# Softmax exponentials on ScalarE without a bias operand, and the matching constant on VectorE

## The chip, the cores and the metric

The kernel runs on one core of one Trainium2 chip. The metric is the device time of one execution in microseconds. The five engines of the core go by the names of the profile: PE (TensorE, matrix products), ACT (ScalarE, activations), DVE (VectorE), POOL (GpSimd) and SP (SyncE, which here only issues transfers). Each engine runs its own queue in order and waits on semaphores for the others. Matrix products are written to PSUM; everything else on the core lives in SBUF.

## The reference

The result is a gated mix of two branches over the same input x (2048 rows, 512 columns, bf16):

```python
x = A_x
g = sigmoid((x * gate_w).sum(-1, keepdims=True))
a = attention(x, A_wqkv, A_wo)
b = state_space(x, B_A_re, ..., B_Dskip)
return g * a + (1 - g) * b

# attention: H = 32 heads of Dh = 16
q, k, v = (x @ wqkv) split into heads
scores = einsum("bhqd,bhkd->bhqk", q, k) * Dh ** -0.5
p = softmax(scores)
o = einsum("bhqk,bhkd->bhqd", p, v);  a = o @ wo

# state_space: per channel d a kernel of 2048 taps, summed over N = 128 complex modes,
K[d, l] = Re(sum_n C[d, n] * exp(dt[d] * A[d, n] * l) * dt[d] * B[d, n])
# convolved causally with the channel of x, plus x * Dskip
```

The scores of 32 heads, 2048 queries and 2048 keys are 134 million exponentials. The change concerns these alone.

## The kernel before, in words

**The attention.** The work is cut into 32 blocks: four chunks of 512 queries, times four sets of eight heads, times the even or the odd heads of a set. In a block four heads are worked on together, and the 2048 keys are taken in 16 tiles of 128. One head, one key tile and 512 queries make a *slot*: 128 x 512 scores, one PSUM bank. There are 2048 slots.

Slots are taken in groups. `qk` (L691) multiplies keys and queries of up to three slots into one of two PSUM tiles of three banks, SC0 and SC1, by turns. `ex` (L704) lets ACT turn two or three of these banks into exponentials in SBUF (ET), as one instruction of 128 x 1024 or 128 x 1536. A group in which ACT takes two banks has a third slot whose exponential DVE computes: `exp_in` (L715) reads the bank, and `exp_out` (L722) ends the work in SBUF (ED). 60 of the 2048 slots go this way. `pv` (L740) multiplies the exponentials of four slots, from ET or from ED, with the values, and adds them up in the PSUM tile OA over the 16 key tiles of a block. The values carry a column of ones, so the same product gives the sum of the exponentials; at a block's end DVE transposes OA and divides by that sum (`norm_a`, `norm_b`, `norm_c`). A factor common to all exponentials of a row thus drops out, but ACT's and DVE's exponentials must have the same factor.

**DVE's exponential.** It writes x / ln 2 as a number whose bits are, read as a float, roughly 2 to that power (L718, into eL as an integer). The mantissa of eL, made into a number m from 1 to 2 (L728), goes into a cubic that corrects the straight line between powers of two (L731, L733, L735). The cubic is worked out with its leading factor POLY[0] divided away, so DVE's result was too large by -1 / (8 * POLY[0]) = ESC = 1.174. ACT's exponential was given the same factor by a bias of ln ESC, which DVE writes once into the tile lnc (L636) and ACT reads as one value for each partition.

**The state space branch and the rest.** The parameters, tables of powers, a chunked scan over 32 chunks of 64 rows and products with it, the gate and the output projection run on DVE, PE and SP between the groups of the attention. Their small products share one PSUM tile, MB, which DVE empties.

**What sets the order.** A planner in the program (`Sched`) writes out the order of each queue before launch. It walks through the groups, charges ACT 0.063 + 0.4267 n us for a group of n slots (L709), and fills the time of PE, DVE, SP and POOL until then with other work by priority. When PE would have too little work, it adds products of zeros (OA<-wm, L1426) up to a budget per group. Buffers get their SBUF addresses at the end, by their size and time of life (`place`, L486). At run time every queue keeps this order.

So a group goes round as follows: PE's `qk` waits until ACT has read the tile of the group before last; ACT's `ex` waits for `qk`; meanwhile PE does `pv` of earlier groups and the other branch's products.

Of the kernel before, what the change touches and what calls it, by code (L numbers as in the profile page):

```python
# [6 lines left out]
FP32 = mybir.dt.float32  # L7
BF16 = mybir.dt.bfloat16
INT32 = mybir.dt.int32
AF = mybir.ActivationFunctionType  # L10
# [6 lines left out]
DH = 16  # L17
# [11 lines left out]
CYCLE, LOWS = 30, 24  # L29
EDGE = 384  # L30
POLY = (-0.10644581, 0.70747665, -1.37730927, 1.77561576)
ESC = -1 / (8 * POLY[0])
EW = 2
VW = 152

# [27 lines left out]
class Prog:  # L63
# [104 lines left out]
    def op(self, eng, fn, R=(), W=(), c=.1, lat=.05, a=0):  # L168
        if self.cap is not None:
            self.cap.append((self.op, (eng, fn, R, W), dict(c=c, lat=lat, a=a)))  # L170
            return
        self.act += a
        self.log.append((self.op, self.q, (eng, fn, R, W)))
        deps = self._deps(eng, R, W)
        i = self.cnt[eng]
        at = self.tm[eng]
        for s, k in deps.items():
            at = max(at, self.fin[(s, k)] + (0 if s == eng else .08))
        self.tm[eng] = at + c
        self.fin[(eng, i)] = at + c + lat  # L180
        self.cnt[eng] += 1
        self._record(eng, fn, deps, eng, i, R, W)
        return at + c + lat
# [197 lines left out]
def declare(nc, es):  # L381
    B = {}

    def sb(name, free, dt=BF16):
        B[name] = Buf(name, "sb", free, dt)


    sb("KT", 4 * S)
    for k in range(16):
        sb(f"Q{k}", 512)  # L390
        sb(f"OnT{k}", 512)
    sb("Qm", 2 * 512)
    sb("VE", 64 * VW)
    sb("ET", NS * 512)
    sb("OT", 512, FP32)
    sb("ON", 512)
    sb("Rz", 2 * 16, FP32)
    sb("Wo", 4 * D)
    sb("xT", 4 * S)
    for n in ("Wk", "Wq", "Wv"):  # L400
        sb(n, 4 * D)
    sb("msk", 2, FP32)
    sb("sgn", 2, FP32)
    sb("hm", 2, FP32)
    sb("piota", 4, FP32)
    sb("hpi", 1, FP32)
    sb("lnc", 1, FP32)
    for k in range(EW):
        sb(f"eL{k}", 512, FP32)
    sb("em", 512, FP32)  # L410
    sb("eu", 512, FP32)
    sb("ED", 4 * 512)

    sb("gwT", 4)
    sb("wm", D)
    sb("x0n", 4 * D)
    sb("idf", P, FP32)
    sb("idb", P)
    sb("gp", NCH, FP32)
    sb("ge", NCH, FP32)  # L420
    sb("g", NCH, FP32)
    sb("g1", NCH, FP32)
    sb("Dpb", 16)
    sb("Dp", 16, FP32)
    sb("Yl", 16 * D)
    sb("fo", 4 * D)
    sb("fp", 4 * D, FP32)

    for n in ("AreT", "AimT", "BreT", "BimT", "CreT", "CimT", "ldt", "dt"):
        sb(n, D)  # L430
    for n in ("an", "bn", "ba", "ea", "e2", "sb_", "cb", "u1", "u2", "u3", "u4", "zr", "zi"):
        sb(n, D, FP32)
    sb("wrb", D)
    sb("nwi", D)
    sb("VV", 2 * D, FP32)
    sb("VL", 2 * D, FP32)
    for n in ("L1", "L2", "L4", "L8", "L16", "L32", "L48"):
        sb(n, 2 * D, FP32)
    sb("MU", 3 * D, FP32)
    sb("pt1", 2 * D, FP32)  # L440
    sb("pt2", 2 * D, FP32)
    for n in ("D16", "D32", "D48"):
        sb(n, 2 * 2 * D)

    sb("FP", 2 * 128 * 8, FP32)
    sb("ft1", 2 * 64 * 8, FP32)
    sb("ft2", 2 * 64 * 8, FP32)
    for k in range(4):
        sb(f"B16{k}", 2 * 128 * 16)

    sb("PT", 2 * 2 * CB * T)
    sb("tt1", 2 * CB * 16)
    sb("tt2", 2 * CB * 16)
    sb("Qt", 2 * 32 * 128)
    sb("Kst", 2 * 8 * P)

    for k in range(NSG):
        sb(f"SG{k}", NCH * 2 * SGH)
    sb("G", 2 * 128, FP32)
    for n in ("s2", "s3"):  # L460
        sb(n, 2 * 128, FP32)

    for k in range(4):
        sb(f"X2{k}", 32 * 64)
        sb(f"XZ{k}", 2 * 32 * 64)
        sb(f"XS{k}", 32 * 64)
        sb(f"XP{k}", 32 * 64)
        sb(f"XR{k}", 32 * 64)

    sb("Py", 3 * 2 * 16 * T)  # L470
    sb("Tt", 3 * 8 * 128)
    for i in range(2):
        B[f"SC{i}"] = Buf(f"SC{i}", "ps", 1536, FP32)
    B["OA"] = Buf("OA", "ps", 512, FP32)
    B["MB"] = Buf("MB", "ps", 512, FP32)
    for n, free in (("ptd", NBLK * P * 2 * CB * T), ("kpd", NBLK * P * 8 * P), ("xrd", S * D)):
        B[n] = Buf(n, "dr", free, BF16)
        B[n].t = nc.dram_tensor("gm_" + n, [free // P, P], BF16)
    for n in ("SC0", "SC1", "OA", "MB"):
        B[n].t = es.enter_context(nc.psum_tensor(n, [P, B[n].free], FP32))  # L480
    for n in ("x", "w", "wo", "are", "aim", "bre", "bim", "cre", "cim", "ldt_d", "dsk_d", "gw_d", "out"):
        B["d_" + n] = Buf("d_" + n, "dr", 1, BF16)
    return B
# [52 lines left out]
def build(nc, A_x, A_wqkv, A_wo, B_A_re, B_A_im, B_B_re, B_B_im, B_C_re, B_C_im, B_log_dt, B_Dskip, gate_w, out):  # L536
    ins = dict(x=A_x.flatten_outer_dims().tensor, w=A_wqkv.tensor, wo=A_wo.tensor, are=B_A_re, aim=B_A_im, bre=B_B_re,
               bim=B_B_im, cre=B_C_re, cim=B_C_im, ldt=B_log_dt.tensor, dsk=B_Dskip.tensor, gw=gate_w.tensor,
               out=out.flatten_outer_dims().tensor)
    with ExitStack() as es:  # L540
        bufs = declare(nc, es)
        prog = Prog(bufs)
        for b in bufs.values():
            b.over, b.order = (), 0
        record(nc, prog, bufs, ins)
        place(nc, bufs)
        log = prog.log
        prog = Prog(bufs)
        for f, q, a in log:
            prog.q = q  # L550
            (prog.op if f.__name__ == "op" else prog.dma)(*a)
        prog.emit(nc, es)
# [10 lines left out]
def record(nc, p, B, ins):  # L563
    KT, Qm, VE, ET, OT, ON, Rz = (B[n] for n in ("KT", "Qm", "VE", "ET", "OT", "ON", "Rz"))
# [4 lines left out]
    op, dma = p.op, p.dma  # L569
    NQ = 512  # L570
    NSL = 4 * NQ
    OFF, GRP, RING, OWN = [], [], {}, {}
# [60 lines left out]
    for k in range(9):  # L633
        mm(lambda: OA(0, [[1, 512]]), lambda: wm(0, [[1, 128]]), lambda: wm(0, [[1, 512]]), [(wm, 0)], [(OA, 0, "warm")])
    op("DVE", lambda v: v.memset(hpi(0, [[1, 1]]), HALF_PI), [], [(hpi, 0)])
    op("DVE", lambda v: v.memset(B["lnc"](0, [[1, 1]]), math.log(ESC)), [], [(B["lnc"], 0)])  # L636
    op("DVE", lambda v: v.memset(pio(1, [[1, 1]]), 0.0), [], [(pio, 1)])
    for k in range(1, 8):
        op("DVE", lambda v, k=k: v.scalar_tensor_tensor(
# [64 lines left out]
    def ex(g):  # L704
        at, d = GRP[g]
        sc, e, n = SC[g % 2], RING[at[0]], len(at)
        op("ACT", lambda a: a.activation(ET(512 * e, [[1, 512 * n]]), sc(0, [[1, 512 * n]]), AF.Exp, scale=DH ** -0.5,  # L707
                                         bias=B["lnc"](0, [[1, 1]])),
           [(sc, i, g) for i in range(n)] + [(B["lnc"], 0)], [(ET, RING[s], s) for s in at], c=.063 + .4267 * n, lat=.1)  # L709

    em, eu, ED = (B[n] for n in ("em", "eu", "ED"))
    r2, r1, r0 = (POLY[i] / POLY[0] for i in (1, 2, 3))
    one = [[1, 512]]

    def exp_in(k, g, d):  # L715
        eL, sc, i = B[f"eL{k % EW}"], SC[g % 2], len(GRP[g][0])
        yield ("DVE", .68, -2)
        op("DVE", lambda v: v.tensor_scalar(eL.int(0, one), sc(512 * i, one), DH ** -0.5 / math.log(2) * 2 ** 23, 124.0 * 2 ** 23 - 2.0 ** 31,  # L718
                                            ALU.mult, ALU.add), [(sc, i, g)], [(eL, 0, d)], c=.68)
        sch.mark(f"ei{k}")  # L720

# [49 lines left out]
    def key(*ns):  # L771
        return [(B[n], 0) for n in ns]
# [588 lines left out]
    for q4 in range(4):  # L1361
        sc = SC[1] if q4 < 3 else MB
# [8 lines left out]
        else:  # L1371
# [6 lines left out]
                                     bias=hpi(0, [[1, 1]])), key("ba") + [(hpi, 0)], key("cb"), c=.6)  # L1378
# [79 lines left out]
    def compose():  # L1458
# [31 lines left out]
        if d is not None:  # L1490
            sch.add(exp_in(nd, g, d), 1)
            sch.add(exp_out(nd, d), 1)
            nd += 1
# [5 lines left out]
    g = 0  # L1499
    while True:  # L1500
        p.q = g
        for s in GRP[g][0]:
            if RING[s] in OWN:
                sch.force(f"pv{OWN[RING[s]] // 4}")
            OWN[RING[s]] = s
        ex(g)
        sch.mark(f"g{g}")
        sch.mark(f"blk{at_slot(GRP[g][0][0])[2]}")
        more = compose()
        if more:  # L1510
            need(g + 1)
            qk(g + 1)
        t = p.tm["ACT"]
        sch.fill(t, .5, zeros, want, quiet())
        lack[0] = max(min(lack[0] + budget() - p.act, 384), 0)
        p.act = lack[1] = 0
        if not more:
            break
        g += 1
# [53 lines left out]
```

## Time and profile before

| what | value |
|---|---|
| median of 3 runs | 991.09 us (981.5 to 995.3) |
| the profiled execution, its own time | 984.66 us |
| its span, first to last instruction | 982.9 us |
| mean granted PE clock | 0.959 |
| busy: ACT | 960.6 us (98%) |
| busy: DVE | 811.3 us (83%) |
| busy: PE | 791.3 us (81%) |
| ACT's exponentials (L707) | 683 instructions, 953.4 us |
| of these 128 x 1536 / 128 x 1024 | 622 / 61 |
| DVE's first pass (L718) | 60 instructions, 41.2 us |

The span lies 1.8 us under the time of its execution. Busy time is the union of an engine's instructions; on ACT and PE neighbouring instructions overlap in the record, so a mean duration is longer than the time from one to the next. A group is named by its source line, engine and operation, then the tiles written <- read, shapes and types, and the count; behind the bar stand busy time, mean duration in ns, and the idle time of the engine just before, with what ended it. All matrix products are issued by one helper line, L578.

### The profile page before, as it was taken

To read this page: it belongs to the slowest core of one execution; us is meant where nothing else is said; L and a number is where in the kernel's file an instruction comes from. 1 tells how busy PE (TensorE), PEld (TensorE's weight loads), DVE (VectorE), ACT (ScalarE), POOL (GpSimd) and SP (SyncE) were. 2 spreads that over 40 slices of the span, in tenths; PEclk is the share of its full clock that TensorE was granted. 3 is DMA by queue.
4 is the path that set the end of the run, shared out by engine and by line. 5 is a ranking of instruction groups with operands and counts; after the bars stand their busy time and mean duration, and the time that the engine had idled before them with its cause. 6 is when DMAs were issued, how large, how long until landed. Compare 5 with 4: busy or idle time off the path is not lost.

```text
span 982.9 us, 17954 instructions
## 1 busy us (share of the span) xinstructions
PE 791.3 (81%) x7409; PEld 269.6 (27%) x7521; DVE 811.3 (83%) x1654; ACT 960.6 (98%) x693; POOL 14.6 (1%) x16
## 2 busy tenths in 40 slices
PE   7888887878777787777888888887788888888884
PEld 3233232212222222212232222323223233333321
DVE  5799989997667888898988788888888987778885
ACT  6999999999999999999999999999999999999995
POOL 4000000000000000010000000000000000000000
PEclk7999999988999989989999779999999999999998
DMA  8300000016767556471242266335312232201100
GB/s 187 87 1 1 1 1 1 1 22 166 178 162 171 151 144 99 133 210 21 55 103 54 58 94 98 83 74 105 58 28 61 79 98 56 55 7 28 33 1 22
DMA packets 171473, 73.40 MB, mean 75 GB/s; under 512 B 150272, under 2 KB 159104, under 8 KB 169344
## 3 DMA queue, kind: packets, MB, share of 16 engines
q1 hardware_dynamic: 169088, 71.07, 31.0%
q10 hardware_dynamic: 2304, 1.18, 0.6%
q8 instruction: 59, 0.97, 0.4%
q14 instruction: 22, 0.18, 0.1%
HBM read 30.02 MB, written 25.17 MB: 56 GB/s over the span
## 4 chain that ended last, share of the span: by engine, by line
ACT 93%; PE 4%; DMA 1%; DVE 1%; issue 0%; ACTq 0%; DVEq 0%
ACT ET L707 93%; PE OA L578 2%; PE SC L578 2%; DMA Wq<-in_A_wqkv_dram 1%; PE MB L578 0%; DVE fo L1253 0%; ACTq L582 0%; DVE OT L752 0%; DVE OnT L762 0%; DVE KT L668 0%; ACT e L826 0%; ACT ea L824 0%; DVE ON L757 0%; DVE Rz L756 0%; ACT ge L1230 0%
## 5 line engine op out<-in xcount | busy, mean ns | idle before, releaser
L707 ACT ACTIVATE ET<-SC,lnc 128x1536 bf16<-128x1536 f32 (+1 forms) x683 | 953.4, 1832 | 6.1 <-PE SC L578 5.6
L578 PE MATMUL SC<-Qm,KT 32*128 32x512 bf16 x2048 | 276.4, 398 | 158.7 <-ACT ET L707 146.0
L578 PE MATMUL OA<-wm 128*128 128x512 bf16 (+9 forms) x684 | 223.3, 374 | 15.4 <-issue 12.8
L578 PE MATMUL OA<-ET,VE 128*32 128x512 bf16 x1988 | 203.9, 402 | 1.8 <-DVE OT L752 1.0
L578 PEld LDWEIGHTS SC<-Qm,KT 32*128 32x128 bf16 x2048 | 66.8, 91 | 382.5 <-ACT ET L707 366.4
L578 PEld LDWEIGHTS OA<-ET,VE 128*32 128x32 bf16 x1988 | 51.0, 94 | 125.0 <-issue 118.3
L578 PEld LDWEIGHTS OA<-wm 128*128 128x128 bf16 x785 | 55.7, 98 | 86.9 <-issue 73.3
L718 DVE TENSOR_SCALAR eL<-SC 128x512 int32<-128x512 f32 x60 | 41.2, 688 | 38.3 <-PE SC L578 38.0
L766 DVE TENSOR_TENSOR tt<-B,D 128x1024 bf16<-128x1024 bf16 x96 | 62.4, 684 | 0.5
L1054 DVE TENSOR_TENSOR SG<-MB,sgn 128x496 bf16<-128x496 f32 x64 | 43.0, 671 | 19.2 <-PE MB L578 18.7
L1087 DVE TENSOR_TENSOR G<-s,s 128x256 f32<-128x256 f32 x120 | 50.7, 423 | 3.3
L578 PE MATMUL MB<-SG,Py 128*64 128x32 bf16 x1024 | 50.9, 230 | 0.0
L1083 DVE TENSOR_TENSOR s<-s,SG 128x256 f32<-128x256 f32 x120 | 50.3, 419 | 0.0
L1077 DVE TENSOR_TENSOR s<-G,MU 128x256 f32<-128x256 f32 x120 | 50.2, 418 | 0.0
L1080 DVE TENSOR_TENSOR s<-G,MU 128x256 f32<-128x256 f32 x120 | 50.2, 418 | 0.0
L735 DVE SCALAR_TENSOR_TENSOR ED<-eu,eL 128x512 bf16<-128x512 f32 x60 | 41.4, 689 | 1.3
L733 DVE SCALAR_TENSOR_TENSOR eu<-eu,em 128x512 f32<-128x512 f32 x60 | 41.3, 688 | 1.4
L752 DVE STREAM_TRANSPOSE OT<-OA 128x512 f32<-128x512 f32 x32 | 22.9, 717 | 23.5 <-PE OA L578 23.0
L731 DVE SCALAR_TENSOR_TENSOR eu<-em 128x512 f32<-128x512 f32 x60 | 41.1, 686 | 0.9
L578 PEld LDWEIGHTS MB<-SG,Py 128*64 128x64 bf16 x1024 | 30.7, 117 | 28.6 <-issue 28.5
L1090 DVE CAST SG<-G 128x256 bf16<-128x256 f32 x120 | 35.4, 295 | 3.2
L766 DVE TENSOR_TENSOR ft<-FP,L 128x1024 f32<-128x1024 f32 (+1 forms) x32 | 34.2, 1086 | 0.4
(137 smaller groups left out, 566.1 us busy)
## 6 DMA issues: line engine op xcount, KB each, us to landing
gm_ptd<-PT SPq DMA_DIRECT2D x16, 1024.0 KB, 5.9
Py<-gm_ptd SPq DMA_DIRECT2D x32, 512.0 KB, 4.1
gm_kpd<-Kst SPq DMA_DIRECT2D x16, 256.0 KB, 3.8
Tt<-gm_kpd SPq DMA_DIRECT2D x128, 32.0 KB, 3.4
gm_xrd<-in_A_x_dram SPq DMA_DIRECT2D x1, 2048.0 KB, 12.1
XS<-gm_xrd SPq DMA_DIRECT2D x8, 256.0 KB, 4.3
XR<-gm_xrd SPq DMA_DIRECT2D x8, 256.0 KB, 4.4
out_dram<-fo SPq DMA_DIRECT2D x28, 64.0 KB, 2.1
```

The lines of the kernel that those rows point to most:

```text
L578: op("PE", lambda t: t.matmul(out(), lhsT(), rhs(), start=start, stop=stop, skip_group_check=True, **kw), R, W, c=c, lat=.15, a=a)
L707: op("ACT", lambda a: a.activation(ET(512 * e, [[1, 512 * n]]), sc(0, [[1, 512 * n]]), AF.Exp, scale=DH ** -0.5, bias=B["lnc"](0, [[1, 1]] ...
L718: op("DVE", lambda v: v.tensor_scalar(eL.int(0, one), sc(512 * i, one), DH ** -0.5 / math.log(2) * 2 ** 23, 124.0 * 2 ** 23 - 2.0 ** 31, A ...
L731: op("DVE", lambda v: v.scalar_tensor_tensor(eu(0, one), em(0, one), r2, em(0, one), ALU.add, ALU.mult), key("em"), key("eu"), c=.69)
L733: op("DVE", lambda v: v.scalar_tensor_tensor(eu(0, one), eu(0, one), r1, em(0, one), ALU.add, ALU.mult), key("em", "eu"), key("eu"), c=.69)
L735: op("DVE", lambda v: v.scalar_tensor_tensor(ED(512 * (d % 4), one), eu(0, one), r0, eL(0, one), ALU.add, ALU.mult), key("eu") + [(eL, 0, ...
L766: op(eng, lambda v: v.tensor_tensor(o(), a(), b_(), f), R, W, c=c)
L1054: op("DVE", lambda v, bank=bank: v.tensor_tensor(sg(2 * SGH + CB * bl + 8 * bank, [[2 * SGH, 31], [SGH, 2], [1, 8]]), MB(0, [[1, 31], [256 ...
L1077: op(e, lambda v: v.tensor_tensor(s2(0, [[128, 2], [1, 128]]), G(0, [[128, 2], [1, 128]]), MU(d0, [[0, 2], [1, 128]]), ALU.mult), key("G", ...
L1080: op(e, lambda v: v.tensor_tensor(s3(0, [[128, 2], [1, 128]]), G(128, [[-128, 2], [1, 128]]), MU(D + d0, [[D, 2], [1, 128]]), ALU.mult), k ...
L1083: op(e, lambda v, so=so: v.tensor_tensor(s2(0, [[128, 2], [1, 128]]), s2(0, [[128, 2], [1, 128]]), sg(so, [[SGH, 2], [1, 128]]), ALU.add), ...
L1087: op(e, lambda v: v.tensor_tensor(G(0, [[1, 256]]), s2(0, [[1, 256]]), s3(0, [[1, 256]]), ALU.add), [(s2, 0), (s3, 0)], [(G, 0)], c=.38)
```

## The change: the factor moves from ACT to DVE

ACT's exponential loses its bias: it computes exp(s x) and no longer exp(s x + ln ESC). The tile lnc and the instruction that fills it go. DVE's first pass adds a constant to the exponent; this constant now holds log2(-8 * POLY[0]) besides 124, so DVE's result is smaller by the factor 1.174 and again agrees with ACT's. The number of instructions on ACT and in DVE's exponential, their shapes and the planner's charges are as before.

```diff
-ESC = -1 / (8 * POLY[0])
+EXP0 = (124 + math.log2(-8 * POLY[0])) * 2 ** 23 - 2.0 ** 31
...
-    sb("lnc", 1, FP32)
...
-    op("DVE", lambda v: v.memset(B["lnc"](0, [[1, 1]]), math.log(ESC)), [], [(B["lnc"], 0)])
...
     def ex(g):
         at, d = GRP[g]
         sc, e, n = SC[g % 2], RING[at[0]], len(at)
-        op("ACT", lambda a: a.activation(ET(512 * e, [[1, 512 * n]]), sc(0, [[1, 512 * n]]), AF.Exp, scale=DH ** -0.5,
-                                         bias=B["lnc"](0, [[1, 1]])),
-           [(sc, i, g) for i in range(n)] + [(B["lnc"], 0)], [(ET, RING[s], s) for s in at], c=.063 + .4267 * n, lat=.1)
+        op("ACT", lambda a: a.activation(ET(512 * e, [[1, 512 * n]]), sc(0, [[1, 512 * n]]), AF.Exp, scale=DH ** -0.5),
+           [(sc, i, g) for i in range(n)], [(ET, RING[s], s) for s in at], c=.063 + .4267 * n, lat=.1)
...
     def exp_in(k, g, d):
-        op("DVE", lambda v: v.tensor_scalar(eL.int(0, one), sc(512 * i, one), DH ** -0.5 / math.log(2) * 2 ** 23, 124.0 * 2 ** 23 - 2.0 ** 31,
+        op("DVE", lambda v: v.tensor_scalar(eL.int(0, one), sc(512 * i, one), DH ** -0.5 / math.log(2) * 2 ** 23, EXP0,
                                             ALU.mult, ALU.add), [(sc, i, g)], [(eL, 0, d)], c=.68)
```

## The prediction

> **What bounds the kernel now.** I read the page first: the busy time of the engines, the chain that ended last by engine, and the costliest group.
>
> ```profile
> span 982.9 us, 17954 instructions
> ...
> PE 791.3 (81%) x7409; PEld 269.6 (27%) x7521; DVE 811.3 (83%) x1654; ACT 960.6 (98%) x693; POOL 14.6 (1%) x16
> ...
> DVE  5799989997667888898988788888888987778885
> ...
> DMA  8300000016767556471242266335312232201100
> ...
> ACT 93%; PE 4%; DMA 1%; DVE 1%; issue 0%; ACTq 0%; DVEq 0%
> ...
> L707 ACT ACTIVATE ET<-SC,lnc 128x1536 bf16<-128x1536 f32 (+1 forms) x683 | 953.4, 1832 | 6.1 <-PE SC L578 5.6
> ```
>
> ACT is busy in 98% of the span and carries 93% of the chain. One line does it: the 683 exponentials of L707, and its idle time before all of them together is 6.1 us. The mean of 1832 ns is not what one costs, since neighbours overlap in the record: 953.4 / 683 is 1.396 us.
>
> Second, the waits, to see who waits for whom.
>
> ```profile
> PE SC L578 <- ACT ET L707: 146.0, 431, 1.0
> ...
> ACT ET L707 <- PE SC L578: 5.6, 6, 3.4
> ```
>
> PE waits for ACT 431 times, ACT for PE six times. So PE has about 146 us to spare and ACT none; a shorter exponential is worth its saving until PE's 146 us, or VectorE's spare time, is used up.
>
> Third, the chain in order of time (start, length, what, how many). It cuts the run into stretches in which one exponential hands over to the next, so a length divided by its count is the true price of one slot.
>
> ```profile
> 14.68 1.54 ACT ET L707
> 16.22 0.52 ACT ea L824
> 16.74 1.43 ACT ET L707
> 18.17 0.56 ACT e L826
> 18.73 178.87 ACT ET L707 x125
> 197.60 0.12 ACT ge L1230
> 197.72 18.61 ACT ET L707 x13
> ...
> 217.31 1.08 PE OA L578 x4
> 218.39 0.54 PE SC L578 x3
> ...
> 225.77 117.54 ACT ET L707 x82
> ...
> 352.36 83.13 ACT ET L707 x58
> ...
> 443.01 109.18 ACT ET L707 x78
> ...
> 567.34 21.43 ACT ET L707 x16
> ...
> 588.78 310.04 ACT ET L707 x227
> 898.83 72.85 ACT ET L707 x55
> ```
>
> 178.87 / 125 is 1.431 us, 117.54 / 82 is 1.433: an exponential over 1536 columns takes a slot of 1.431 us (the later stretches are shorter per slot because some of theirs have 1024 columns). The counts add up to 656 with the two of the start. The other 27 lie in four gaps where the chain runs through PE: 216.33 to 225.77, 343.31 to 352.36, 435.49 to 443.01 and 552.20 to 567.34, together 41.2 us.
>
> What these gaps are, the windows show (length, then busy us and counts of PE, PEld, DVE, ACT and POOL, then PE clock and DMA).
>
> ```profile
> 213.60:227.30 13.70, 13.23 (x65) 2.53 (x65) 12.74 (x20) 13.06 (x10) 0.34 (x1) 0.50 0.00 1
> ...
> core 0: 982.9 us, clock 0.959
> ```
>
> The granted clock was 0.50 there; a group then costs PE 0.54 + 1.08 = 1.62 us, more than an ACT slot. A mean clock of 0.959, if it is made of 1.00 and 0.50, means 2 x 0.041 x 982.9 = 81 us at half clock.
>
> **The change part by part.** *The bias operand.* All 683 exponentials lose it; rows, columns, source and target stay. To price it I need ACT instructions that differ in little else.
>
> ```profile
> L707 ACT ACTIVATE ET<-SC,lnc 128x1536 bf16<-128x1536 f32 x622 | 907.7, 1875 | 5.9 <-PE SC L578 5.4
> L707 ACT ACTIVATE ET<-SC,lnc 128x1024 bf16<-128x1024 f32 x61 | 79.3, 1398 | 0.2 <-PE SC L578 0.2
> ...
> L1377 ACT ACTIVATE cb<-ba,hpi 128x512 f32<-128x512 f32 x1 | 0.7, 705 | 0.0
> L826 ACT ACTIVATE e<-an 128x512 f32<-128x512 f32 x1 | 0.7, 665 | 0.0
> ...
> L1375 ACT ACTIVATE sb__131<-bn 128x512 f32<-128x512 f32 x1 | 0.6, 629 | 0.0
> L824 ACT ACTIVATE ea<-an 128x512 f32<-128x512 f32 x1 | 0.6, 620 | 0.0
> L1370 ACT CAST xT<-SC 128x512 bf16<-128x512 f32 x1 | 0.6, 586 | 1.7 <-PE SC L578 1.7
> ```
>
> The names right of the arrow show who reads a bias: ET has lnc, cb has hpi, and ea, e and sb_ have none. The instructions of ACT in order of time (start, length) add which of them began beside another.
>
> ```profile
> 8.77 0.63 ACT L1375 ACTIVATE sb__131<-bn 128x512 f32<-128x512 f32 x1
> 9.31 0.70 ACT L1377 ACTIVATE cb<-ba,hpi 128x512 f32<-128x512 f32 x1
> ...
> 16.12 0.62 ACT L824 ACTIVATE ea<-an 128x512 f32<-128x512 f32 x1
> ```
>
> cb begins before sb_ ends at 9.40, and ea before the first ET ends at 14.68 + 1.54 = 16.22, both by about 0.1 us. They have one shape and one type, so the pair is alike but for the bias and the function: 705 - 620 = 85 ns. cb against sb_, both sines, gives 76.
>
> A duration isn't a slot, so I check with the chain. Two slots without a bias, ge (32 columns) and ea (512), give (0.52 - 0.12) / 480 = 0.833 ns a column, and so a fixed part of 0.52 - 0.427 = 0.093 us. ET's fixed part is 1.431 - 1.280 = 0.151. The difference, 58 ns, is the lower end: it would be right if reading PSUM began no sooner than reading SBUF. But CAST, which reads PSUM, took 586 against ea's 620, so a bias-free read of PSUM may be 34 ns shorter still, which makes 92. The upper end is the first ET, 1540, less what CAST would take for as many columns, 586 + 1024 x 0.833 = 1439: 101 ns, by another operation and from an idle engine. I take 85, since its two rows differ in the operand and the function alone; 58 and 101 stay for the range. The new slots are then 1.346 us for 1536 columns and about 0.92 for 1024.
>
> The Trainium skill, "ScalarE: Activation LUTs", section "What ACT_TABLE_LOAD costs", gives 93 ns for each pointer operand and an overlap of 93 ns between neighbours; its slot with a bias would have a fixed part of 280 - 93 = 187, where this trace shows 151. By its 93 the sum below would be 925.
>
> On ACT's queue nothing moves and no wait is added. The wait of the first exponential for the constant's memset goes, and was long over: the memset ran at 1.4 us, the exponential at 14.68.
>
> *The memset of lnc.*
>
> ```profile
> L636 DVE MEMSET lnc<- x1: 59/59/59, 1.4 to 1.4; 128x1 f32 x1
> ...
> DVE xT L1372 <- PE SC L578: 1.5, 1, 1.5
> ```
>
> It goes: 59 ns of VectorE, which soon after waits 1.5 us for PE in any case. I cost it at nothing; uncovered it is 0.06 us.
>
> *The constant of VectorE's first pass.* Another number in the same instruction of the same shape, 60 times: nothing, and without an operand changed I see no way to a cost. The rest of the cubic is untouched.
>
> *The order of the queues.* It is planned with a charge of 0.063 + 3 x 0.4267 = 1.343 us for a group (L709), which the change leaves alone. So instructions stay in their places, the PE filler among them, and the order is one laid out for a cadence that ACT now misses by 88 ns and would then nearly keep. SBUF addresses may shift by one 32-byte buffer; I cost that at nothing.
>
> *The sum*, against the profiled execution's own 984.66 us. ACT's 656 slots on the chain: 656 x 0.085 = 55.8 us, which leaves 928.9. The 27 in the gaps give nothing, because PE sets the pace there. The rest of the half-clock time, 81 - 41 = 40 us, lies under ACT today, at least in part; at most 28 slots would lose their gain to PE, 2.4 us, and I take half, 1.2. That gives **930**. The median of the three runs shown, 991.09, is 6 us over this execution, inside their own spread of 981.5 to 995.3; less than 2% of it is no change that a measurement of this kernel can tell.
>
> What is late next? PE's spare 146 us less 56 leaves about 90. VectorE's stretches of most work are these.
>
> ```profile
> 175.00:200.00 25.00, 20.45 (x197) 6.51 (x197) 23.59 (x38) 25.00 (x20) 0.00 (x0) 1.00 0.13 21
> 200.00:225.00 25.00, 20.24 (x120) 4.69 (x121) 24.11 (x35) 24.87 (x18) 0.34 (x1) 0.77 0.01 2
> ```
>
> 25 us shrink to 25 x 1.346 / 1.431 = 23.5. VectorE's own work in them, 23.59 and 24.11 us, no longer fits by 0.1 and 0.6 us; both have lag to give, as what it does there is mostly preparation for a later stage. The DMA digits stay at 7 or below behind the start, so a 6% quicker cadence leaves the transfers room.
>
> **The rivals.**
>
> *The bias hardly shows in a slot (58 ns).* For it: the hand-over on the chain, which is the thing that repeats. Against it: CAST's shorter read. 984.66 - 656 x 0.058 + 1.2 = **948**.
>
> *VectorE becomes the bound.* In the nine slices with a digit of 9, 9 x 24.6 = 221 us, PE would stand before tiles that VectorE hasn't read, and ACT behind it: the 154 slots there keep 1.431, which costs 13.1: **943**. For it: 94% to 96% of these stretches is work already. Against it: ACT loses only 5.6 us to PE today, and the queue order assumes 1.343.
>
> *The half clock goes away.* PE would do the same work in 6% less time; if that keeps the clock up, the four gaps shrink to 27 x 1.346 = 36.3 us, 4.9 less, and the 1.2 falls away: **924**. For it: the gaps follow a stretch of sparse PE work in at least one case (the row from 200 to 225 has 120 matmuls, the one before 197). The Trainium skill, "TensorE: Matmul & The Clock Gate", section "What's actually happening", says that the throttled state is the default and that activity releases it. By that rule this rival is right in direction; against it, no row here shows where the limit lies.
>
> *The change doesn't do it.* An instruction without a bias might still fetch a zero from SBUF, or the fetch might lie under the end of the instruction ahead: no gain, **985**. Against it: ea and e name no such tile and are 40 to 85 ns shorter than cb, and ea's slot right behind an ET has 0.093 where ET's has 0.151.
>
> *Slower: the half clock spreads.* A group in the gaps took 41.2 / 27 = 1.52 us, set by PE whatever ACT does. Each slot moved to that state loses 1.52 - 1.346 = 0.18 us, so some 310 further slots, nearly half of the run, eat the gain of 55.8; if all 656 go over, the time is 930 + 656 x 0.18 = **1048**. For it: it happens already in 81 us, and the trace doesn't say why. Against it: nothing takes work from PE.
>
> **How the numbers follow.** The forecast of 930 gets 0.60, the 58 ns 0.10, VectorE 0.12, the clock that stays up 0.10, no gain 0.05, slower 0.03. The range: its low end has 101 ns on all 683 slots, 984.66 - 69.0 = 916, with a little of the clock's gain: 914. Its high end is the 58 ns case with 2 us of VectorE's lateness: 950. Outside lie no gain, slower, and the worst of VectorE on a small saving. Faster by over 2% are all but the last two cases, 0.92; within 2% 0.05; slower 0.03.
>
> **What would show it.** In the changed profile the L707 group should read ET<-SC alone, with near 683 x 85 = 58 us less busy time, about 895; in the chain the stretch from 18.7 should hold about 125 slots in 168 us. A stretch still at 1.43 at full clock refutes the price; at 1.37 the 58 ns are right. ACT's wait for PE should stay under some 10 us and PE's for ACT fall toward 90; if the first grows to tens, or the chain shows VectorE's transposes and evacuations in the slices with a 9, VectorE is the bound. The forecast is wrong above all if the clock differs: half-clock time well over 81 us, or none.

## The result, and the profile after

The changed kernel takes 922.29 us, median of 4 runs (920.91 to 923.37), where the kernel before takes 993.19 in the runs beside it (981.5 to 999.22). The ratio is 0.932, with an interval of 0.924 to 0.941; it compares fast runs alone, so 999.22, over 1.5% above the fastest run of its kernel, is not in it. The profiled execution took 923.37 us against 984.66, so 61.3 us less.

The page of the changed kernel, the lines that answer to those shown of before:

```profile
span 921.6 us, 18065 instructions
...
PE 788.7 (86%) x7521; PEld 266.4 (29%) x7521; DVE 807.1 (88%) x1653; ACT 900.0 (98%) x693; POOL 14.6 (2%) x16
...
PEclk9999999999899999999999999999999999999998
...
ACT 87%; DVE 7%; PE 3%; DMA 2%; issue 0%; ACTq 0%; SPq 0%; DVEq 0%
...
L705 ACT ACTIVATE ET<-SC 128x1536 bf16<-128x1536 f32 (+1 forms) x683 | 892.8, 1836 | 5.5 <-PE SC L577 5.5
```

The exponentials read SC alone now. Their busy time fell from 953.4 to 892.8 us, by 60.6: nearly the whole gain stands in this one row. ACT is still busy in 98% of the span and still waits only some 5 us for PE. The row of the clock has one slice below 9 between the first and the last, where before had six:

```profile
PEclk7999999988999989989999779999999999999998
```

PE and VectorE do the same work in a shorter span, so their shares rise, to 86% and 88%.

The chain of the changed kernel in order of time (start, length, what, how many):

```profile
14.63 1.45 ACT ET L705
16.08 0.52 ACT ea L821
16.60 1.34 ACT ET L705
17.93 0.56 ACT e L823
18.50 143.70 ACT ET L705 x107
162.25 0.39 PE SC L577 x3
...
233.87 0.70 DVE PT L763
...
240.69 293.58 ACT ET L705 x221
534.31 0.39 PE SC L577 x3
...
536.15 300.44 ACT ET L705 x235
```

143.70 / 107 is 1.343 us, against 1.431 before: **88 ns less for each slot**. ea, which never had a bias, keeps its 0.52.

Between 162 and 236 us the chain runs mostly through VectorE. That doesn't mean that ACT stood still. The chain is followed back from the end; at 236 us it finds PE held up by an evacuation of VectorE's, and from there back it follows VectorE's queue and one transfer. The windows of the changed kernel show ACT's part (length; busy us of PE, PEld, DVE, ACT, POOL with counts; clock):

```profile
150.00:175.00 25.00, 21.97 (x175) 6.33 (x174) 23.61 (x33) 25.00 (x21) 0.00 (x0) 1.00 0.00 1
175.00:200.00 25.00, 20.63 (x185) 6.17 (x181) 24.31 (x39) 25.00 (x21) 0.00 (x0) 1.00 0.14 22
200.00:225.00 25.00, 20.71 (x157) 5.38 (x157) 20.33 (x37) 25.00 (x20) 0.34 (x1) 1.00 0.33 111
225.00:250.00 25.00, 20.00 (x173) 5.99 (x172) 19.50 (x34) 23.39 (x18) 0.00 (x0) 0.86 0.87 201
```

ACT is busy through all of it up to 225 us, with 20 or 21 exponentials in 25 us. VectorE is at 97% from 175 to 200, just short of being the bound. Only the last row has a gap, 1.6 us.

### The profile page after: what moved, and what is told of

Same layout as the page of the kernel before. It is cut to its first block, busy times and chain, and to the rows that moved or that the text cites. A ratio compares the mean times of both kernels' runs of the same rounds, so it can differ in the third digit from the quotient of the medians.

```text
span 921.6 us, 18065 instructions
## 1 busy us (share of the span) xinstructions
PE 788.7 (86%) x7521; PEld 266.4 (29%) x7521; DVE 807.1 (88%) x1653; ACT 900.0 (98%) x693; POOL 14.6 (2%) x16
## 4 chain that ended last, share of the span: by engine, by line
ACT 87%; DVE 7%; PE 3%; DMA 2%; issue 0%; ACTq 0%; SPq 0%; DVEq 0%
ACT ET L705 87%; DVE ft L763 2%; DVE tt L763 2%; PE OA L577 1%; PE SC L577 1%; DMA gm_ptd<-PT 1%; DMA Wq<-in_A_wqkv_dram 1%; DVE PT L763 1%; PE MB L577 1%; DVE B L763 1%; DVE FP L763 0%; DVE fo L1250 0%; DVE B L944 0%; DVE XP L1178 0%; DVE FP L921 0%
## 5 line engine op out<-in xcount | busy, mean ns | idle before, releaser
L705 ACT ACTIVATE ET<-SC 128x1536 bf16<-128x1536 f32 (+1 forms) x683 | 892.8, 1836 | 5.5 <-PE SC L577 5.5
L577 PE MATMUL SC<-Qm,KT 32*128 32x512 bf16 x2048 | 267.7, 386 | 110.2 <-ACT ET L705 91.6
L577 PE MATMUL OA<-wm 128*128 128x512 bf16 (+8 forms) x785 | 242.0, 367 | 2.6 <-DVE OT L749 1.4
L577 PE MATMUL OA<-ET,VE 128*32 128x512 bf16 x1988 | 198.3, 391 | 1.7 <-DVE OT L749 1.0
```

The source lines that it names most:

```text
L577: op("PE", lambda t: t.matmul(out(), lhsT(), rhs(), start=start, stop=stop, skip_group_check=True, **kw), R, W, c=c, lat=.15, a=a)
```

## The experiments

**One. The bias as a number in the instruction.** The kernel before, with ACT's bias no longer fetched but kept:

```diff
-    sb("lnc", 1, FP32)
...
-    op("DVE", lambda v: v.memset(B["lnc"](0, [[1, 1]]), math.log(ESC)), [], [(B["lnc"], 0)])
...
-                                         bias=B["lnc"](0, [[1, 1]])),
+                                         bias=math.log(ESC)),
...
```

> The kernel before with one edit: the bias ln ESC is written into the instruction as a number, and the tile lnc and its memset go; VectorE's constant stays as it was. Theory (what costs is the fetch of an operand from SBUF, once for each exponential): slots of 1.343 us as in the changed kernel and a time of 920 to 925 us, so the edit on VectorE was needed for nothing but the arithmetic. Rival (adding a bias costs ACT time in itself, and half the gain came from leaving out the addition): slots between 1.36 and 1.43, time of 940 us or more.

Measured: 921.63 us (921.1 to 923.88), ratio 0.934 (0.930 to 0.939). Its chain:

```profile
12.21 1.45 ACT ET L705
13.66 0.52 ACT ea L822
14.17 1.34 ACT ET L705
...
16.08 143.69 ACT ET L705 x107
```

143.69 / 107 is 1.343 again. The addition costs nothing; what cost 88 ns is the operand read from lnc. A wait for lnc's memset can't be it: the program writes out a wait only where it isn't already known to be over (`_record`, L141), so that one stands once and not 683 times. The edit on VectorE is needed only because the factor has to go somewhere: as a number in ACT's instruction it is as cheap.

**Two. All of the change but the fetch.** The changed kernel's VectorE constant, and a bias of 0.0 that ACT reads from lnc:

```diff
-ESC = -1 / (8 * POLY[0])
+EXP0 = (124 + math.log2(-8 * POLY[0])) * 2 ** 23 - 2.0 ** 31
...
-    op("DVE", lambda v: v.memset(B["lnc"](0, [[1, 1]]), math.log(ESC)), [], [(B["lnc"], 0)])
+    op("DVE", lambda v: v.memset(B["lnc"](0, [[1, 1]]), 0.0), [], [(B["lnc"], 0)])
...
```

> The changed kernel, but ACT reads a bias of zero from SBUF: the whole of the change in arithmetic, VectorE's constant among it, without the operand's removal. Theory (the fetch costs): slots of 1.431 us as before, a time like that of the kernel before, ratio 0.99 to 1.01. Rival (VectorE's constant, another layout of SBUF or another order brought a part): ratio below 0.98.

Measured: 986.26 us against 986.43 of the kernel before on the same chip, ratio 0.999 (0.996 to 1.002). Its chain has the old slot, 178.87 / 125 = 1.431:

```profile
16.60 178.87 ACT ET L707 x125
```

So VectorE's constant brings nothing and costs nothing, and a bias of zero is as dear as any other if it is fetched.

**Three. Two operands.** Experiment two, with the scale from SBUF too:

```diff
+    sb("scl", 1, FP32)
...
+    op("DVE", lambda v: v.memset(B["scl"](0, [[1, 1]]), DH ** -0.5), [], [(B["scl"], 0)])
...
-... AF.Exp, scale=DH ** -0.5,
+... AF.Exp, scale=B["scl"](0, [[1, 1]]),
...
```

> The same, and the scale read from SBUF too: two fetched operands for each exponential. Theory (each fetch adds its own 88 ns to a slot): slots of 1.52 us, 683 x 0.088 = 60 us more than with one, time 1040 to 1060 us. Rival (operands are fetched together, so the second is free): slots of 1.43 us, ratio 0.99 to 1.01.

Measured: 1062.9 us (1061.16 to 1071.27), ratio 1.077 (1.071 to 1.084). The chain, and below it the clock of the same execution:

```profile
13.70 0.52 ACT ea L826
14.22 1.52 ACT ET L709
...
16.31 188.88 ACT ET L709 x124
```

```profile
core 0: 1069.2 us, clock 0.837
```

A slot is 188.88 / 124 = 1.523 us, 92 ns more than with one operand: each has its own price. But 683 x 0.092 is 63 us, and the time rose by 76.6 against experiment two, beyond the 1060 that I had given as the most. The other 14 us come with a lower clock: 0.837 to 0.872 in the five runs, where experiment two has 0.940 to 0.961. That is the mechanism of my slower rival, met on the way to longer slots instead of shorter ones.

**Four and five. The clock apart from the slot.** If PE's density in time sets the clock, it can be moved by the filler alone. The kernel before with more filler:

```diff
-FILL = 1400
+FILL = 1492
```

> The kernel before with the budget of PE filler raised by the ratio of the slots, from 1400 to 1492 columns, so that PE does as many columns in a microsecond as in the changed kernel; ACT still fetches its bias. Theory (the half clock went because PE's work became denser in time): mean clock about 0.99, slots still 1.431, time about 980 us, 5 to 15 us under the kernel before on the same chip, with less spread. Rival (the clock has another cause): clock 0.95 to 0.97 and the time of the kernel before.

Measured: 982.94 us (980.35 to 992.57), ratio 0.997 (0.993 to 1.000). The clock was 0.957 to 0.991 in ten runs, with a middle of 0.981, where the 19 runs of the kernel before on that chip have 0.925 to 0.975 with a middle of 0.951. The clock moved as the theory says, if not all the way. The time moved by 3.5 us, less than the 5 I had given as the least, and its interval just reaches 1, so a gain in time isn't shown.

The changed kernel with less filler:

```diff
-FILL = 1400
+FILL = 1314
```

> The changed kernel with the budget of PE filler lowered from 1400 to 1314 columns a group, so that PE does about as many columns in a microsecond as in the kernel before; ACT's exponentials stay without a fetched operand. Theory (the half clock follows how dense PE's work is in time): mean clock falls from 0.99 to 0.95 to 0.97, the exponential's slot stays at 1.343 us, and the time rises by 3 to 15 us over 922. Rival (the clock follows the length of a slot, or something else that the operand brought): clock 0.99 and 920 to 923 us.

Measured: 933.14 us (923.69 to 935.99), ratio 0.942 (0.935 to 0.950), clock 0.951 to 0.980. Its page:

```profile
PEclk9999999989899899997599999999999999999997
```

and a stretch of its chain that still gives 143.70 / 107 = 1.343 a slot:

```profile
17.52 143.70 ACT ET L705 x107
```

So the short slots don't keep the clock up by themselves; with less filler the half clock came back, the time rose by about 11 us, and the exponentials of this stretch at full clock are no dearer. One of the four runs, at a clock of 0.980, took only 923.69 us.

Both experiments fit the theory that the density of PE's work sets the clock. They don't isolate it: the planner lays out all queues anew around another filler. In experiment four, for one, the first step G<-s,s of the scan begins at 311.8 us, in the kernel before at 333.8.

**Six. More filler still**, in the changed kernel, 1492 for 1400.

> The changed kernel with the budget raised from 1400 to 1492 columns. Theory: the clock is near 1 already, so at most 1 us is gained, and PE may lose as much in its full stretches: 920 to 926 us. Rival (half clock still costs several us in the changed kernel): below 918 us.

Measured: 921.91 us (921.62 to 923.04), clock 0.986 to 0.993. Nothing is left to gain there; 1400 is enough at the new cadence. Against this run, on the same chip, experiment five is 11.2 us slower.

**Seven to nine. Is ACT alone still the bound, and how near is VectorE?** More slots for VectorE shorten ACT's work. First, VectorE's exponentials during the scan of the last quarter too:

```diff
-... for r in range(4)):
+... for r in range(3)):
```

> The changed kernel with VectorE's exponentials allowed during the scan of the last quarter too: 69 groups in which ACT takes two banks where there were 61, 614 with three where there were 622. If ACT alone sets the time, 8 x 0.427 = 3.4 us less: 919 us. If VectorE has no room in that scan, its lateness reaches ACT through PE: 922 us or more.

Measured: 977.15 us, ratio 0.989 (0.983 to 0.995): 55 us slower than the changed kernel, far worse than either number I had given. The last windows of its trace (columns as above), and its last step of the scan, an addition of which each quarter has 30:

```profile
875.00:900.00 25.00, 23.22 (x271) 8.75 (x271) 16.83 (x32) 25.00 (x21) 0.00 (x0) 1.00 0.20 54
900.00:925.00 25.00, 17.24 (x278) 11.52 (x278) 4.06 (x9) 6.41 (x6) 0.00 (x0) 0.69 0.34 89
925.00:950.00 25.00, 15.58 (x132) 10.04 (x128) 7.74 (x16) 0.00 (x0) 0.00 (x0) 0.50 0.18 43
```

```profile
L1084 DVE TENSOR_TENSOR G<-s,s x120: 382/424/429, 315.6 to 876.6; 128x256 f32<-128x256 f32 x120
```

ACT is done between 906 and 907 us (6.41 us of work after 900), earlier than in the changed kernel. But the scan ends at 877 us, where in the changed kernel, below, the same row gives 741.7. VectorE's exponentials rank ahead of the scan in the planner (their steps have -2 and 2.5, the scan 3, and of two that can start at once the lower goes first) and crowd it out, and the products and outputs that need it follow after the attention, at half clock and with ACT idle beside them.

```profile
L1084 DVE TENSOR_TENSOR G<-s,s x120: 382/425/430, 315.3 to 741.7; 128x256 f32<-128x256 f32 x120
```

Second, a further buffer ED, so that a second set of four slots, one of the next block, can begin before the first is used:

```diff
-    sb("ED", 4 * 512)
+    sb("ED", 8 * 512)
...
-            if quads and f"dp{quads[-1]}" not in sch.flag:
+            if len(quads) > 1 and f"dp{quads[-2]}" not in sch.flag:
...
```

> As the run before, and VectorE's exponentials of a second set of four slots may begin while the first set waits to be used (a second buffer ED): 77 groups with two banks, 606 with three. If ACT alone sets the time, 16 x 0.427 = 6.8 us less than the changed kernel: 915 us. If VectorE, 88% busy in the changed kernel, is the bound by then: 922 us or more.

Measured: 995.48 us, ratio 1.006 (1.002 to 1.010), with the edit of experiment seven in it. The same row of its scan ends later still, at 910.6 us; why the second buffer delays it further stays open. Third, the buffer alone, with the scans left in peace:

> The changed kernel with the second buffer ED alone, and no exponentials of VectorE during a scan, as in the changed kernel: 65 groups with two banks, 618 with three. If ACT alone sets the time and the scans keep their place, 4 x 0.427 = 1.7 us less than the changed kernel on the same chip: about 920.5. If VectorE's time is full, no gain or some us more.

Measured: 922.4 us (920.41 to 923.37). The 1.7 us didn't come.

**Ten. The changed kernel again**, beside experiment nine.

> The changed kernel as it is, on the same chip as the run before it and with the same runs of the kernel before: 920 to 924 us, ratio 0.930 to 0.937, mean clock about 0.99.

Measured: 922.36 us (920.95 to 923.46), ratio 0.934 (0.931 to 0.938), clock 0.987 to 0.993. No version that was run beats the changed kernel; experiments one, six and nine equal it.

## Why the prediction was right, point by point

The forecast was 930 in a range of 914 to 950; 922.29 was measured, and 923.37 in the profiled execution. The direction, the place and the mechanism of the price held. What the forecast assumed of the clock did not: it kept today's half clock, and the measured time lies nearest to the 924 of the rival in which the half clock goes, which I had given 0.10. The sum was 6.7 us too careful for that execution, and its terms say where:

| term | forecast | measured | difference |
|---|---|---|---|
| price of the fetched operand in a slot | 85 ns | 88 ns | 656 x 0.003 = 2.0 us |
| slots in the four gaps at half clock | no gain from 27 | gaps gone | 27 x 0.088 = 2.4 us |
| further slots lost to the half clock | 1.2 us | none | 1.2 us |
| other idle time of ACT | unchanged | about 1 us less | 1.0 us |

The last row comes from the stretch from the first exponential's start to the last one's end: 957.0 us before (14.68 to 971.68) and 896.0 after (14.63 to 910.61, where PE's last product of the chain begins), so 61.0 less; the slots explain 683 x 0.088 = 60.1. Only the price in the first row and this stretch are measured; the second and third rows are the forecast's own terms, priced at 88 ns because the four gaps are no longer in the chain. A new stretch at half clock, from 234.9 to 241.7, in which ACT stood idle for 1.6 us, is inside the 896.0.

**The price.** Of the ways to get it, the pair of durations, 705 - 620 = 85, came nearest. That was partly luck: the other pair of the same kind, the two sines, gave 76, and 58 with CAST's 34 gave 92. The lower end, 58 ns, took ea's fixed part of 0.093 us for that of a bias-free exponential. The groups by form of the changed kernel show why it failed:

```profile
L705 ACT ACTIVATE ET<-SC 128x1536 bf16<-128x1536 f32 x622 | 849.3, 1892 | 5.5 <-PE SC L577 5.5
L705 ACT ACTIVATE ET<-SC 128x1024 bf16<-128x1024 f32 x61 | 72.1, 1267 | 0.0
...
L1370 ACT ACTIVATE dt<-ldt 128x512 bf16<-128x512 bf16 x1 | 0.6, 630 | 0.2 <-DMA ldt<-in_B_log_dt_dram 0.2
...
L821 ACT ACTIVATE ea<-an 128x512 f32<-128x512 f32 x1 | 0.6, 622 | 0.0
L1367 ACT CAST xT<-SC 128x512 bf16<-128x512 f32 x1 | 0.6, 585 | 2.0 <-PE SC L577 2.0
```

ea reads SBUF. An exponential that reads PSUM has a fixed part of 1.343 - 1.280 = 0.063 us in its slot, 30 ns less than ea's 0.093; CAST's shorter duration had told of 34. ea also writes f32 where ET writes bf16, but that isn't it: dt writes bf16 from SBUF and takes 630 ns, no less than ea. No run changes the source alone. The upper end, 101, was too much by 13: the first exponential alone lost 1.54 - 1.45 = 0.09 us. The Trainium skill, "ScalarE: Activation LUTs", section "What ACT_TABLE_LOAD costs", had 93 ns for each pointer operand. Its figures, less the overlap that it gives, make an estimate of 187 ns for the slot's fixed part with one operand and 93 without. The traces nearly agree on the price, 88 for the first and 92 for the second, and agree on the slot of ea, which reads SBUF; on PSUM they show 151 and 63, not 187 and 93.

**The clock.** I gave the rival that the half clock goes away 0.10 and let the forecast keep the gaps. It went: a mean of 0.990 where it was 0.959. Time at half clock fell from about 81 us to 2 x 0.010 x 921.6 = 18. What I had for it was one sparse stretch. These are the windows of the kernel before: the 13 us ahead of each of its four gaps, a dense window at full clock, and two more at full clock:

```profile
200.20:213.60 13.40, 9.11 (x69) 2.50 (x66) 12.91 (x18) 13.40 (x11) 0.00 (x0) 1.00 0.01 2
330.00:343.30 13.30, 9.79 (x109) 3.37 (x110) 11.08 (x28) 13.30 (x11) 0.00 (x0) 1.00 0.66 219
422.00:435.50 13.50, 9.29 (x80) 2.52 (x73) 13.02 (x38) 13.50 (x11) 0.05 (x1) 1.00 0.89 256
538.00:551.60 13.60, 10.30 (x121) 3.85 (x119) 10.16 (x19) 13.60 (x11) 0.34 (x1) 1.00 0.18 49
100.00:113.40 13.40, 11.55 (x88) 3.60 (x88) 11.78 (x17) 13.40 (x11) 0.00 (x0) 1.00 0.00 1
...
247.80:261.20 13.40, 9.61 (x111) 3.38 (x111) 6.99 (x13) 13.40 (x10) 0.00 (x0) 1.00 0.76 242
...
238.10:326.20 88.10, 64.58 (x612) 20.56 (x617) 66.98 (x115) 88.10 (x63) 0.34 (x1) 1.00 0.72 162
```

PE was busy for 68% to 76% ahead of the gaps, and for 86% in the dense window. But a low share doesn't foretell the half clock: the last two windows are as sparse, 72% and 73%, and the clock was 1.00 through all 88 us of the longer one. So the gaps follow sparse work, and not all sparse work is followed by a gap. The changed kernel has one half-clock stretch between its first exponential and its last, from 234.9 to 241.7, and it too follows a sparse one:

```profile
221.50:234.90 13.40, 9.73 (x77) 2.77 (x77) 11.00 (x18) 13.40 (x11) 0.00 (x0) 1.00 0.99 170
...
234.90:241.70 6.80, 5.78 (x39) 1.51 (x39) 3.79 (x7) 5.20 (x4) 0.00 (x0) 0.50 0.87 289
```

Experiments four and five moved the mean clock both ways by the filler, and three moved it down by longer slots. So denser work goes with a higher clock; at what density PE loses it, no run shows. The rule of the Trainium skill that I cited against keeping the gaps ("TensorE: Matmul & The Clock Gate", section "What's actually happening") was right in direction.

How much of the whole gain is the clock's? In the 19 runs of the kernel before beside experiments one to four, the time goes with the clock: 992.78 us at 0.925, 980.50 at 0.975. Experiment four reached 980.35 at 0.991. So an undisturbed clock leaves the old kernel at about 980, and 980 - 921.6 = 58 to 59 us are the operand's, near the 60.1 of the slots. The rest of the distance between the medians, 6 us on that chip and about 10 in the first comparison without its run of 999.22, would be the clock's. The 58 to 59 are read off single runs and not a comparison of their own; a straight line through the 19 runs, carried on to a clock of 0.99, gives 976, and then the operand's share is 54.

**VectorE.** It did not become the bound, but came near. Its busiest window rose to 24.31 of 25 us and ACT stayed busy all through it; the 13.1 us of that rival weren't lost. Where it decides, experiment seven shows: eight exponentials of VectorE's, at the wrong place in its queue, cost 55 us.

**No gain.** Refuted by experiment one, in which the bias is there but not fetched, together with two, in which it is fetched but zero.

**Slower.** It had the direction of the clock wrong: with quicker slots PE does the same work in less time, and the time at half clock shrank. Experiment three, with longer slots and a lower clock, is the same argument run backwards.

**The order of the queues.** ACT's slot now equals the planner's charge of 1.343 us, so ACT keeps almost the planned cadence. PE's waits for ACT fell from 146.0 to

```profile
PE SC L577 <- ACT ET L705: 91.6, 298, 1.0
...
ACT ET L705 <- PE SC L577: 5.5, 6, 3.3
```

91.6 us, which the forecast had put at about 90, and ACT's for PE stayed at 5.5. Late in the run PE leads for some groups even at full clock: in the window from 836.60 it was busy for 5.36 of 5.40 us.

```profile
836.60:842.00 5.40, 5.36 (x47) 1.80 (x48) 5.13 (x10) 4.98 (x5) 0.00 (x0) 1.00 0.13 29
```

That makes PE, with VectorE beside it, a likely next limit; no run here tests which comes first.

## What to carry to other kernels

Where one engine is busy all the time with many like instructions, read the fixed part of its slot off the chain (length of a stretch by its count, less the columns), and look for what in the instruction it pays for: here one per-partition operand for each of 683 instructions was 6% of the run, and a number in the instruction does the same for nothing. Take the comparison instruction from the same memory as the one to be priced; pricing an exponential that reads PSUM by ea, which reads SBUF, hid 30 of the 88 ns. And when a change makes the bounding engine quicker, ask what the denser work may do to the clock of PE, before charging today's stretches of half clock to the new kernel as well.

## What was not expected

When the forecast was made, nothing told how closely the clock would follow the filler: a budget 6% lower, met by fewer columns of zeros, took its mean in the changed kernel from 0.99 to about 0.955 and cost 11 us, while 7% more brought nothing. And the second fetched operand, worth 63 us by its slots, cost 76.6, with a lower clock beside it: a longer slot thins PE's work. In this kernel, bound by ACT, a slot's price had a second price on PE behind it; neither the row of the group nor the chain at full clock shows it.
